# Block sums on GpSimd, stores in other queues, later seeds: an attention and gated-MLP kernel

## The chip, the cores and the metric

One core of a Trainium2 chip runs the whole kernel. The metric is the device time of one execution in microseconds, the median of several runs. The kernel runs five engines beside each other: TensorE (PE, matmuls), VectorE (DVE), ScalarE (ACT), GpSimd (POOL) and SyncE (SP). DMAs are issued by SP, ACT or POOL, each in the order in which they stand on that engine.

## The reference

The output mixes an attention branch s and a gated MLP branch g: `x + s * g`. All data is fp32, 2048 rows by 512 columns.

```python
xn = _layernorm(x, axis=-1)
s = _A_ref(xn, A_wqkv, A_wo)      # 32 heads of 16; each row attends to 8 rows, 2 apart
g = _silu(_B_ref(xn, B_w_in, B_w_sp, B_b_sp, B_w_out))
return x + s * g

# _B_ref
z = _gelu(jnp.einsum("bsd,df->bsf", x, w_in))          # w_in: 512 x 1792
z1 = z[..., :Fh]                                       # Fh = 896
z2 = _layernorm(z[..., Fh:], axis=-1)
g = jnp.einsum("ts,bsf->btf", w_sp, z2) + b_sp[None, :, None]   # w_sp: 2048 x 2048
return jnp.einsum("bsf,fd->bsd", z1 * g, w_out)
```

## The kernel before

**Precision.** Each fp32 operand is split into a high half (ScalarE copies it, L192, tile names end in h) and a low half (VectorE subtracts, L193, names end in l). A product takes three matmuls: high by high, high by low, low by high (L709 to 711, L801, L1036 to 1038).

**Stages of TensorE**, in order: q, k, v (to about 141 us of the span); z1 (first half of w_in, to 226); z2 (second half, the "second projection", to 300); the spatial product of w_sp and z2 (to 582); the projection b by w_out (to 658); the projection s of the attention's output by wo (to 706).

**The spatial product** is done by blocks with seven instead of eight products, each for two column halves of the output (a = 0, 1): m1, m2, m6, m7, m4, m5, m3. `block_product` goes over 8 row blocks of weights, two in a step, and after a step runs what `steps` lists. Weights are rows of w_sp as they are (`plain`, tiles wsp_*) or sums of blocks (`summed`, tiles ws_*) that were stored earlier to sums_d. A product adds onto PSUM banks that ScalarE seeds with a bias or with minus an earlier product (`seed`, L819).

**The block sums** come in eight sets (1, i) of interest here. In the kernel before, GpSimd adds sets 0 to 4 early, in the qkv stage (`pool_sums`, L389, loads and stores through its own queue). VectorE adds sets 5 and 6 in the z2 stage (`raw_sums`, tiles sr_*, their buffers shared with the raw weights, four in all; loads by SP, stores by ACT). GpSimd adds set 7 in m1a (`late_sums`).

**z2 stage.** Per row block j: gelu from PSUM into a tile zt_j (ScalarE, L712), statistics (VectorE, L721), reciprocal deviation (GpSimd, L723 to 726), normalisation (ScalarE, L730), split. `combine` (L743) then takes differences of the tiles zt_i and zt_(i+8) and stores two pieces to t_d, L749 and L750, read back later as operands of m4 to m7. The zt tiles share eight buffers with block sums and others (`t4`): a new tile waits for the last reader of the old one, a store too. In the program as built zt_10 follows zt_0 in one buffer.

**Attention** runs on VectorE through nearly the whole span, 16 units of two steps (products L561 and L605, reductions L568). GpSimd does the first fold of each (L616) and stores the result to o_d (L630). `load_o` brings it back as tiles ol_g_k, four pieces each, split into o_k for the projection s.

**What sets the order.** A framework schedules the program from priorities and its own cost estimates; it fixes the order on each engine before the run. `pin` keeps some instructions in program order. A change in one place can therefore move instructions elsewhere. The gates z1 * g are stored to g_d (`stored_gates`) and read back ahead of the projection b.

Of the kernel before, what the change touches and what calls it, by code (L numbers as in the profile page):

```python
# [57 lines left out]
def kernel(  # L58
# [12 lines left out]
):  # L71
    nc = tc.nc
    pins = [True]
    lows, sums_of = [], []

    def pin(ins):
        return tc.keep_in_program_order(ins) if pins[0] else ins
# [112 lines left out]

    def split(hi, lo, src):
        first_ = pin(nc.scalar.activation(hi, src, AF.Copy))  # L192
        lows.append(pin(nc.vector.tensor_tensor(lo, src, hi.bitcast(F32), op=ALU.subtract)))  # L193
        return first_

# [205 lines left out]
    def raw_sums(a, i):  # L401
        ts = [
            fetch(w_sp[2 * a + c, r + i], CT, f"sr_{a}_{i}_{c}_{r}") for r in (0, HT) for c in range(2)
        ]
        added(ts, nc.vector)
        for n, t in enumerate(ts):
            nc.scalar.dma_start(sums_d[a, n // 2, i, :, n % 2], t)

    def early_tile(name):
        return t2(name).rearrange("p (i t) -> p i t", i=2)  # L410
# [63 lines left out]
    for j in range(11, NT):  # L474
        if j + 2 < NT:
            fetch_cols(j + 2)
        turned = column_tile(j)
        if j == 12:
            for i in range(HT - 3):
                pool_sums(1, i, early_tile, turned, SYNC)  # L480
        low_x(j - 1, cols[j - 1])
        if j % 2:
            pair(0, j - 5)
# [233 lines left out]
    def z2_stats(j, zt):  # L717
        st = const.tile([P, 2, 6], F32, tag="st2", name=f"zst_{j}", bufs=3)
        mv, nm = mvz[:, j], nmz[:, j : j + 1]
        for h in range(2):  # L720
            nc.vector.bn_stats(st[:, h], zt[:, h * FQ : (h + 1) * FQ])  # L721
        nc.vector.bn_aggr(mv, st)
        nc.gpsimd.tensor_tensor(nm, mv[:, 0:1], mone, op=ALU.mult)  # L723
        nc.gpsimd.tensor_scalar(mv[:, 1:2], mv[:, 1:2], EPS, None, op0=ALU.add)
        nc.gpsimd.tensor_tensor(mv[:, 1:2], mv[:, 1:2], nhalf, op=ALU.pow)
        return nc.gpsimd.tensor_tensor(nm, nm, mv[:, 1:2], op=ALU.mult)  # L726

    def z2_normal(j, zt, n):
        zh, zl = z2_at(j)
# [5 lines left out]
    def combine(i, zts):  # L735
        b11, b12, b21, b22 = [z[:, p_] for z in zts for p_ in (first_part, last_part)]
        for out_, p_, q_, op in (
            (b11, b11, b12, ALU.subtract),
            (b12, b12, b22, ALU.subtract),
            (b22, b22, b11, ALU.add),  # L740
            (b21, b21, b22, ALU.subtract),
        ):
            nc.vector.tensor_tensor(out_, p_, q_, op=op)  # L743
        split(*[t[:, ODD + 1 :] for t in z2_at(i)], blocks(b22, ODD))
        v = b11
        src = bass.AP(
            tensor=v.tensor, offset=v.offset, ap=[list(v.ap[0]), [FH - F3, 2], [1, F3]]
        )
        nc.scalar.dma_start(t_d[:2, i].rearrange("a p t -> p a t"), src)  # L749
        nc.scalar.dma_start(t_d[2, i], b21)  # L750

    early_pair = [wts.tile([P, CT], F32R, tag=f"w{n}", name=f"wsp_0_0{n}") for n in "hl"]
    split(*early_pair, fetch(w_sp[0, 0], CT, "wsp_0_0"))
# [6 lines left out]
    raw_z = {}  # L760
    for i in range(HT + 2):
        if i in (1, 3):
            raw_sums(1, HT - 3 + i // 2)
        if i < HT:
            raw_z[i] = [t4(f"zt_{j}").rearrange("p i t -> p (i t)")[:, :FH] for j in (i, HT + i)]
            for h in range(2):
                for j, zt in zip((i, HT + i), raw_z[i]):
                    z2_half(j, h, zt)
                if i == HT - 1 and h == 0:
                    spatial[0, 1] = spatial_block(0, 1)  # L770
        if 0 < i <= HT:
            for j, zt in zip((i - 1, HT + i - 1), raw_z[i - 1]):
                rows_known = z2_stats(j, zt)
        if i > 1:
            for j, zt, n in zip((i - 2, HT + i - 2), raw_z[i - 2], (ODD + 1, FB)):
                z2_normal(j, zt, n)
            combine(i - 2, raw_z[i - 2])

    def load_o(g, k, i=None):
        ot = raws.tile([P, D], F32, tag="raw", name=f"ol_{g}_{k}", bufs=RAW)  # L780
        for q in range(P // Q):
            a, b = divmod(q, CS // Q)
            pin(nc.sync.dma_start(
                ot[q * Q : (q + 1) * Q].rearrange("c (a x) -> c a x", a=P // Q),
                o_d[2 * k + a, g, :, b].rearrange("(a c) x -> c a x", c=Q),
            ))
# [29 lines left out]
        banks[a, f] = mm(f"g_{a}_{f}")  # L816

    def seed(a, f, src, scale=1.0):
        nc.scalar.activation(banks[a, f], src, AF.Copy, scale=scale)  # L819

    def evict(a, f, out_):
        nc.scalar.activation(out_, banks[a, f], AF.Copy)
# [25 lines left out]
    def summed(a, half_, i):  # L848
        return lambda s: prep(sums_d[a, half_, s, :, i], CT, f"ws_{a}{half_}{i}_{s}")
# [26 lines left out]
    def later(fn, *args):  # L876
        return lambda: fn(*args)
# [5 lines left out]
    def stored_gates(a, f0):  # L883
        zl = z1_pair(2 * a, f0, 2)
        n = min(2, ODD - f0)
        xl = t4(f"xl_{a}_{f0}", n)
        nc.sync.dma_start(xl, x_d[a, f0 : f0 + n].rearrange("f p t -> p f t"))
        for f in (f0, f0 + 1):
            times(zl[:, f - f0], banks[a, f], zl[:, f - f0])
            if f < ODD:  # L890
                seed(a, f, xl[:, f - f0], -1.0)
        nc.scalar.dma_start(g_d[a, f0 : f0 + 2].rearrange("f p t -> p f t"), zl)

    def gated(c, f, src, zt):
        times(zt, src, zt)
# [58 lines left out]
        for f in range(ODD + 1):  # L954
            seed(1, f, biases[1][0])

    def late_sums(i):
        return later(pool_sums, 1, i, t4, rows_known, NOSYNC)

    block_product(  # L960
        0, "m1a", at(0, 0), plain(0, 0, 0), odd(0),
        steps=(
            [second_bias, late_sums(HT - 1)], [], [second_seeds], []
        ),
    )
    oo = t4("oo")
# [2 lines left out]
    def kept(a):  # L969
# [14 lines left out]
    )  # L984
    stored_gates(0, 0)
    stored_gates(0, 2)
    block_product(1, "m2b", at(1, 0), plain(1, 0, 1), odd(1))
    stored_gates(1, 0)
    stored_gates(1, 2)
    block_product(  # L990
        0, "m6a", at(0, LAST), summed(0, 0, 0), steps=([T4[0]], [T4[1]], [T4[2]], [T4[3]])
    )
    spill(0)
    block_product(1, "m6b", at(0, LAST), summed(1, 0, 0))
# [147 lines left out]
```

## Time and profile before

| | |
|---|---|
| time, median of 3 runs | 709.67 us (707.76 to 713.64) |
| the profiled execution | 712.41 us, span 710.6 us, mean granted clock 0.992 |
| PE busy | 693.5 us (98%), 3084 matmuls |
| DVE busy | 610.0 us (86%), 878 |
| ACT busy | 284.3 us (40%), 458 |
| POOL busy | 216.7 us (30%), 246 |
| DMA | 182.38 MB, mean 257 GB/s |

Times in rows of the profile are microseconds from the start of the span. A row of the timeline gives start, duration, engine, line, operation and tiles (buffer numbers left out), and in brackets how long the engine stood idle before it and what ended that. A row of waits gives who waited for whom: total, times, longest. L12 is line 12 of the kernel before.

### The profile page before, as it was taken

To read this page: it belongs to the slowest core of one execution; us is meant where nothing else is said; L and a number is where in the kernel's file an instruction comes from. 1 tells how busy PE (TensorE), PEld (TensorE's weight loads), DVE (VectorE), ACT (ScalarE), POOL (GpSimd) and SP (SyncE) were. 2 spreads that over 40 slices of the span, in tenths; PEclk is the share of its full clock that TensorE was granted. 3 is DMA by queue.
4 is the path that set the end of the run, shared out by engine and by line. 5 is a ranking of instruction groups with operands and counts; after the bars stand their busy time and mean duration, and the time that the engine had idled before them with its cause. 6 is when DMAs were issued, how large, how long until landed. Compare 5 with 4: busy or idle time off the path is not lost.

```text
span 710.6 us, 9238 instructions
## 1 busy us (share of the span) xinstructions
PE 693.5 (98%) x3084; PEld 575.9 (81%) x3084; DVE 610.0 (86%) x878; ACT 284.3 (40%) x458; POOL 216.7 (30%) x246
## 2 busy tenths in 40 slices
PE   8999999999999989989999989999999999999996
PEld 7888888888888979967788878888888888888885
DVE  6775387998999999997999999999998999997445
ACT  4343332332433463865444435432343453213421
POOL 3104594522334557536122112142210111320000
PEclk9999999999999999999999999999999999999998
DMA  8759999879999672556798858576659675444896
GB/s 267 257 182 339 337 371 338 249 222 396 310 397 390 233 255 83 180 201 237 264 383 315 312 171 295 194 247 231 217 186 310 189 240 196 151 168 140 281 294 240
DMA packets 106177, 182.38 MB, mean 257 GB/s; under 512 B 9168, under 2 KB 49360, under 8 KB 106128
## 3 DMA queue, kind: packets, MB, share of 16 engines
q1 hardware_dynamic: 56608, 97.42, 40.8%
q0 software_dynamic: 12224, 48.05, 19.4%
q10 hardware_dynamic: 37296, 36.31, 15.0%
q8 instruction: 24, 0.39, 0.2%
q14 instruction: 25, 0.20, 0.1%
HBM read 122.42 MB, written 59.32 MB: 256 GB/s over the span
## 4 chain that ended last, share of the span: by engine, by line
PE 55%; DVE 18%; DMA 14%; issue 7%; ACT 3%; POOL 1%; SPq 1%; ACTq 0%; DVEq 0%
PE g L801 25%; PE qkv L383 5%; PE qkv L381 5%; PE qkv L382 5%; PE b L1038 3%; PE b L1037 3%; PE b L1036 3%; DVE lg L568 3%; DMA sg<-b_d 3%; DVE pr L561 2%; DMA x<-in_x 2%; DMA z_d<-z1t 2%; DVE BIG L193 2%; DVE pv L605 2%; DMA sb<-in_w_sp 1%
## 5 line engine op out<-in xcount | busy, mean ns | idle before, releaser
L616 POOL TENSOR_TENSOR pv<-pv 128x1024 f32<-128x1024 f32 x29 | 69.6, 2399 | 87.9 <-DVE pv L605 87.9
L561 DVE TENSOR_TENSOR pr<-k,q 128x2048 f32<-128x2048 f32 x32 | 74.3, 2322 | 8.9 <-DMA q<-qkv_d 5.3
L605 DVE TENSOR_TENSOR pv<-v,lg 128x2048 f32<-128x2048 f32 x32 | 73.2, 2287 | 1.4 <-DMA v<-qkv_d 0.9
L568 DVE TENSOR_REDUCE lg<-pr 128x128 f32<-128x2048 f32 x32 | 72.9, 2278 | 0.1
L630 POOL DMA_DIRECT2D o_d<-tt x32 | 18.0, 564 | 175.5 <-DVE tt L629 175.3
L429 ACT ACTIVATE stage<-qkv 128x512 f32<-128x512 f32 x36 | 21.4, 596 | 49.5 <-PE qkv L383 44.6
L709 PE MATMUL z<-w_0h,BIG 128*128 128x512 f32 x64 | 25.8, 403 | 2.2 <-ACT zt L712 2.2
L621 DVE TENSOR_TENSOR pv<-pv 128x512 f32<-128x512 f32 x32 | 22.9, 715 | 3.6 <-POOL pv L616 3.5
L710 PE MATMUL z<-w_0l,BIG 128*128 128x512 f32 x64 | 25.7, 401 | 0.0
L730 ACT ACTIVATE zt<-zt,nmz,mvz 128x896 f32<-128x896 f32 x16 | 18.0, 1132 | 19.0 <-POOL nmz L726 18.9
L711 PE MATMUL z<-w_0h,BIG 128*128 128x512 f32 x64 | 25.5, 399 | 0.0
L540 POOL DMA_DIRECT2D k<-qkv_d x13 | 7.3, 560 | 55.6 <-DVE pr L561 55.6
L276 DVE TENSOR_TENSOR xT<-xT,mr 128x512 f32<-128x512 f32 x20 | 13.8, 688 | 11.7 <-DMA mr<-mv_d 6.9
L1047 ACT ACTIVATE bt<-b 128x512 f32<-128x512 f32 x16 | 9.5, 596 | 33.5 <-PE b L1038 33.5
L710 PE MATMUL z<-w_1l,BIG 128*128 128x384 f32 x64 | 21.6, 337 | 0.7 <-DVE w_1l L193 0.7
L192 ACT ACTIVATE BIG<-zl 128x512 fp32r<-128x512 f32 x20 | 12.4, 628 | 24.4 <-DVE zl L871 24.4
L193 DVE TENSOR_TENSOR BIG<-zt,BIG 128x512 fp32r<-128x512 f32 (+2 forms) x24 | 19.8, 826 | 2.4 <-ACT BIG L192 2.4
L711 PE MATMUL z<-w_1h,BIG 128*128 128x384 f32 x64 | 21.5, 336 | 0.0
L709 PE MATMUL z<-w_1h,BIG 128*128 128x384 f32 x64 | 21.5, 335 | 0.0
L389 POOL TENSOR_TENSOR sb<-sa,sb 128x512 f32<-128x512 f32 x12 | 16.8, 1402 | 11.3 <-DMA sb<-in_w_sp 10.9
L801 PE MATMUL g<-ws_1h,BIG 128*128 128x512 f32 x52 | 20.1, 389 | 0.0
L801 PE MATMUL g<-ws_3h,BIG 128*128 128x512 f32 x52 | 20.1, 389 | 0.0
(475 smaller groups left out, 2304.5 us busy)
## 6 DMA issues: line engine op xcount, KB each, us to landing
qkv_d<-stage ACTq DMA_DIRECT2D x24, 512.0 KB
v<-qkv_d POOLq DMA_DIRECT2D x14, 704.0 KB, 4.9
k<-qkv_d POOLq DMA_DIRECT2D x13, 704.0 KB, 5.9
sums_d<-sa POOLq DMA_DIRECT2D x14, 512.0 KB, 6.4
sums_d<-sb POOLq DMA_DIRECT2D x14, 512.0 KB, 7.3
z_d<-z1t ACTq DMA_DIRECT2D x14, 512.0 KB
zl<-z_d SPq DMA_DIRECT2D x12, 512.0 KB
tr<-t_d SPq DMA_DIRECT2D x12, 384.0 KB
```

The source lines that it names most:

```text
L193: lows.append(pin(nc.vector.tensor_tensor(lo, src, hi.bitcast(F32), op=ALU.subtract)))
L381: nc.tensor.matmul(pq, xh[:, k], wh, start=k == 0, stop=False)
L382: nc.tensor.matmul(pq, xh[:, k], wl, start=False, stop=False)
L383: nc.tensor.matmul(pq, xl[:, k], wh, start=False, stop=k == KB - 1)
L561: line(nc.vector.tensor_tensor(pr, taps(ks[u], j0), qb.unsqueeze(1).to_broadcast([P, W, NJ * CS]), op=ALU.mult))
L568: line(nc.vector.tensor_reduce(lgs[u][:, :, j0 * HS : (j0 + NJ) * HS], pr.rearrange("p w (i d) -> p w i d", d=DH), axis=AX.X, op=ALU.add,))
L605: line(nc.vector.tensor_tensor(pv.rearrange("p w (i d) -> p w i d", d=DH), taps(vs[u], j0).rearrange("p w (i d) -> p w i d", d=DH), lgs[u] ...
L616: eng.tensor_tensor(pv[:, 0:4], pv[:, 0:4], pv[:, 4:8], op=ALU.add)
L709: nc.tensor.matmul(pz, xh[:, k], wh, start=k == 0, stop=False)
L710: nc.tensor.matmul(pz, xh[:, k], wl, start=False, stop=False)
L711: nc.tensor.matmul(pz, xl[:, k], wh, start=False, stop=k == KB - 1)
L801: nc.tensor.matmul(pg, z[a], w[b], start=start and i == 0, stop=stop and i == 2, skip_group_check=seeded)
```

## The change

Three things:

1. GpSimd adds six sets early instead of five; VectorE adds sets 6 and 7 in the z2 stage; the late set on GpSimd, and the tiles it took, are gone.
2. Stores move between queues: those of `raw_sums` (8) and of `combine` (16) from ACT's to SP's, those of `stored_gates` (4) from ACT's to GpSimd's. Of the four loads of each ol tile, two move from SP's to GpSimd's queue.
3. The seeds of `stored_gates` are collected and issued in step 2 of the next block product, ordered behind the last high half that was split by then.

```diff
-    lows, sums_of = [], []
+    lows, highs, sums_of = [], [], []
@@ split
         first_ = pin(nc.scalar.activation(hi, src, AF.Copy))
+        highs.append(first_)
@@ raw_sums
-            nc.scalar.dma_start(sums_d[a, n // 2, i, :, n % 2], t)
+            nc.sync.dma_start(sums_d[a, n // 2, i, :, n % 2], t)
@@ the qkv stage
-            for i in range(HT - 3):
+            for i in range(HT - 2):
                 pool_sums(1, i, early_tile, turned, SYNC)
@@ combine
-        nc.scalar.dma_start(t_d[:2, i].rearrange("a p t -> p a t"), src)
-        nc.scalar.dma_start(t_d[2, i], b21)
+        nc.sync.dma_start(t_d[:2, i].rearrange("a p t -> p a t"), src)
+        nc.sync.dma_start(t_d[2, i], b21)
@@ the z2 loop
-            raw_sums(1, HT - 3 + i // 2)
+            raw_sums(1, HT - 2 + i // 2)
@@ load_o
-            pin(nc.sync.dma_start(
+            pin((nc.gpsimd if b else nc.sync).dma_start(
@@ stored_gates
             if f < ODD:
-                seed(a, f, xl[:, f - f0], -1.0)
-        nc.scalar.dma_start(g_d[a, f0 : f0 + 2].rearrange("f p t -> p f t"), zl)
+                awaited.append((a, f, xl[:, f - f0], -1.0))
+        nc.gpsimd.dma_start(g_d[a, f0 : f0 + 2].rearrange("f p t -> p f t"), zl)
+
+    awaited = []
+
+    def seeds():
+        for args in awaited:
+            tc.add_manual_dep(
+                seed(*args).ins, highs[-1].ins.name, NOSYNC, reason="behind the weights"
+            )
+        awaited.clear()
@@ the block products
-            [second_bias, late_sums(HT - 1)], [], [second_seeds], []
+            [second_bias], [], [second_seeds], []
...
-    block_product(1, "m2b", at(1, 0), plain(1, 0, 1), odd(1))
+    block_product(1, "m2b", at(1, 0), plain(1, 0, 1), odd(1), steps=([], [seeds], [], []))
...
-        0, "m6a", at(0, LAST), summed(0, 0, 0), steps=([T4[0]], [T4[1]], [T4[2]], [T4[3]])
+        0, "m6a", at(0, LAST), summed(0, 0, 0),
+        steps=([T4[0]], [T4[1], seeds], [T4[2]], [T4[3]]),
```

In the changed program as built zt_11 follows zt_0 in one buffer, and zt_10 follows sa_0_7, a tile of the block sums (0, i).

How the order moves is shown at three places. In the names, numbers behind the last underscore only count tiles.

The start of m1a, on TensorE (g_0_0 and g_0_1 are its first two column blocks, wsp_0_s its weights, L951, now L961, writes zeros for m1b). Before, the one group ran on to the sixth weight:

```order
L801 MATMUL g_0_0_3224<-wsp_0_4l_3313,BIG_98 128x512
L801 MATMUL g_0_0_3224<-wsp_0_4h_3312,BIG_98 128x512
L951 MATMUL g_1_2_3230<-BIG_98 128x512
L801 MATMUL g_0_0_3224<-wsp_0_5h_3318,BIG_98 128x512
L801 MATMUL g_0_1_3225<-wsp_0_0h_2474,BIG_98 128x512
L801 MATMUL g_0_1_3225<-wsp_0_0l_2475,BIG_98 128x512
```

```order
L802 MATMUL g_0_1_3235<-wsp_0_4h_3312,BIG_98 128x512
L802 MATMUL g_0_0_3234<-wsp_0_4l_3313,BIG_98 128x512
L802 MATMUL g_0_0_3234<-wsp_0_4h_3312,BIG_98 128x512
L802 MATMUL g_0_1_3235<-wsp_0_4l_3313,BIG_98 128x512
L802 MATMUL g_0_1_3235<-wsp_0_4h_3312,BIG_98 128x512
L961 MATMUL g_1_3_3241<-BIG_98 128x512
L802 MATMUL g_0_0_3234<-wsp_0_5h_3318,BIG_98 128x512
L802 MATMUL g_0_1_3235<-wsp_0_5h_3318,BIG_98 128x512
```

Now the second column block takes its first five weights ahead of the first matmul with wsp_0_5h. On ScalarE the seed of g_0_1 and the two gelus of zt_15 have moved ahead of the split of wsp_0_5, and the table load and the exponential of lg_6 behind it. In SP's queue the stores of t_d and of the sums now stand between the loads of these weights.

The end of m2b on VectorE (ws_100_s are m6b's weights, pv_8_0 and lg_9 the attention's). Before:

```order
L599 TENSOR_TENSOR lg_8_1509<-lg_8_1509,sm_8_1575 128x256
L605 TENSOR_TENSOR pv_8_0_1579<-v_4_0_1573,lg_8_1509 128x2048
L568 TENSOR_REDUCE lg_9_1553<-pr_9_4_1566 128x8x16
L583 MEMSET lg_9_1553 1x8
L583 MEMSET lg_9_1553 1x16
L193 TENSOR_TENSOR ws_100_0l_4041<-ws_100_0r_4038,ws_100_0h_4040 128x512
L193 TENSOR_TENSOR ws_100_1l_4047<-ws_100_1r_4044,ws_100_1h_4046 128x512
```

```order
L194 TENSOR_TENSOR ws_100_0l_4041<-ws_100_0r_4038,ws_100_0h_4040 128x512
L194 TENSOR_TENSOR ws_100_1l_4047<-ws_100_1r_4044,ws_100_1h_4046 128x512
L630 STREAM_TRANSPOSE tt_7_4_1580<-pv_7_4_1571 128x256
L598 TENSOR_REDUCE sm_8_1585<-lg_8_1519 128x32
L599 RECIPROCAL sm_8_1585<-sm_8_1585 128x32
L600 TENSOR_TENSOR lg_8_1519<-lg_8_1519,sm_8_1585 128x256
L606 TENSOR_TENSOR pv_8_0_1589<-v_4_0_1583,lg_8_1519 128x2048
L569 TENSOR_REDUCE lg_9_1563<-pr_9_4_1576 128x8x16
```

The low halves of the first two weights now stand ahead of the product and the reduction.

The end, in SP's queue (ol_2_* is the last group of the attention's output, out stores results). Before:

```order
L783 DMA ol_2_2_6092<-o_d_84 32x4x128 x4
L783 DMA ol_2_3_6101<-o_d_84 32x4x128 x3
L1097 DMA out_0<-sg_4_5898 128x1024
L1059 DMA x3_10_6040<-in_x 128x1024
L783 DMA ol_2_3_6101<-o_d_84 32x4x128
L1097 DMA out_0<-sg_6_5933 128x1024
```

```order
L784 DMA ol_2_2_6092<-o_d_84 32x4x128 x2
L784 DMA ol_2_3_6101<-o_d_84 32x4x128 x2
L1105 DMA out_0<-sg_2_5858 128x1024
L1067 DMA x3_8_6005<-in_x 128x1024
L1066 DMA sg_10_6039<-b_d_76 128x1024
L1105 DMA out_0<-sg_4_5898 128x1024
```

SP's two pieces of ol_2_3 now stand ahead of two more stores of results; its other two are in GpSimd's queue, behind the attention's last store.

More of the change, by code (lines that the diff above doesn't have):

```diff
@@ L725, in z2_stats @@
         nc.gpsimd.tensor_tensor(mv[:, 1:2], mv[:, 1:2], nhalf, op=ALU.pow)
-        return nc.gpsimd.tensor_tensor(nm, nm, mv[:, 1:2], op=ALU.mult)
+        nc.gpsimd.tensor_tensor(nm, nm, mv[:, 1:2], op=ALU.mult)
     def z2_normal(j, zt, n):
@@ L772 @@
             for j, zt in zip((i - 1, HT + i - 1), raw_z[i - 1]):
-                rows_known = z2_stats(j, zt)
+                z2_stats(j, zt)
         if i > 1:
@@ L818, in seed @@
     def seed(a, f, src, scale=1.0):
-        nc.scalar.activation(banks[a, f], src, AF.Copy, scale=scale)
+        return nc.scalar.activation(banks[a, f], src, AF.Copy, scale=scale)
     def evict(a, f, out_):
@@ L955, in second_seeds @@
             seed(1, f, biases[1][0])
-    def late_sums(i):
-        return later(pool_sums, 1, i, t4, rows_known, NOSYNC)
     block_product(
```

## The prediction

> **What bounds the kernel now.** I read the page first, then the waits of PE, then the slices in which PE stood still, then the rows around each stall.
>
> ```profile
> PE 693.5 (98%) x3084; PEld 575.9 (81%) x3084; DVE 610.0 (86%) x878; ACT 284.3 (40%) x458; POOL 216.7 (30%) x246
> PE g L801 <- ACT wsp_5h L192: 2.4, 1, 2.4
> ...
> PE g L801 <- DVE ws_0l L193: 2.2, 1, 2.2
> PE g L801 <- ACT wsp_7h L192: 1.0, 1, 1.0
> ```
>
> TensorE is busy 98% of the span and the change takes no matmul away, so only time in which PE waits or runs slowly can be won. Its waits behind the opening are a handful: four of 2.2 to 2.4 us (two more of them stand in the brackets of rows below) and one of 1.0. The slices show that a wait costs more than itself (columns: width, then PE, PEld, DVE, ACT, POOL busy with counts, granted clock, DMA share, GB/s).
>
> ```profile
> 260.00:270.00 10.00, 7.81 (x32) 6.52 (x31) 8.88 (x14) 5.58 (x11) 3.99 (x4) 0.83 0.47 173
> 300.00:310.00 10.00, 7.60 (x28) 5.78 (x28) 10.00 (x13) 9.94 (x17) 3.78 (x4) 0.86 0.53 172
> 350.00:360.00 10.00, 10.00 (x45) 8.29 (x45) 9.97 (x12) 7.57 (x13) 1.50 (x2) 1.00 1.04 349
> 410.00:420.00 10.00, 7.84 (x35) 6.18 (x34) 9.00 (x14) 3.91 (x7) 2.37 (x1) 1.00 0.62 195
> ```
>
> Undisturbed, 45 matmuls of 512 columns start in 10 us, one each 0.222 us. Behind the waits at 260 and 304 us the granted clock falls to 0.83 and 0.86 and matmuls start further apart; behind the one at 411 us it stays 1.00.
>
> ```profile
> 260.12 0.39 PE L711 MATMUL z<-w_0h,BIG 128*128 128x512 f32 x1
> 262.70 0.80 PE L709 MATMUL z<-w_0h,BIG 128*128 128x512 f32 x1 [2.19 <-ACT zt L712]
> ...
> 266.22 0.40 PE L711 MATMUL z<-w_0h,BIG 128*128 128x512 f32 x1
> 304.24 0.39 PE L951 MATMUL g<-BIG 128*128 128x512 f32 x1
> 307.03 0.76 PE L801 MATMUL g<-wsp_5h,BIG 128*128 128x512 f32 x1 [2.40 <-ACT wsp_5h L192]
> ...
> 310.60 0.39 PE L801 MATMUL g<-wsp_2l,BIG 128*128 128x512 f32 x1
> 411.26 0.84 PE L801 MATMUL g<-ws_0h,BIG 128*128 128x512 f32 x3
> 414.26 0.50 PE L801 MATMUL g<-ws_0l,BIG 128*128 128x512 f32 x1 [2.16 <-DVE ws_0l L193]
> 692.97 0.39 PE L1038 MATMUL s<-BIG,o_2l 128*128 128x512 f32 x1
> 695.54 0.50 PE L1036 MATMUL s<-BIG,o_3h 128*128 128x512 f32 x1 [2.18 <-ACT o_3h L192]
> ...
> 699.75 0.40 PE L1037 MATMUL s<-BIG,o_2h 128*128 128x512 f32 x1
> ```
>
> Nine starts from 260.12 to 266.22 should take 9 x 0.222 = 2.0 us and take 6.10: 4.1 lost in the second projection. Nine from 304.24 to 310.60: 4.4 lost in the first block product, m1a. Three from 411.26 to 414.26: 2.3 lost in m6b. Eleven from 692.97 to 699.75: 4.3 lost in the last projection, s. With the 1.0 us for wsp_7h that is 16.1 us, or 2.3% of the kernel. Beyond waits under 1 us, the change cannot bring more than this, whatever else it moves.
>
> **Second projection.** What is late at 262.70 is a gelu, and the gelu waits for its tile:
>
> ```profile
> 256.20 0.55 DVE L743 TENSOR_TENSOR zt<-zt,zt 128x384 f32<-128x384 f32 x1
> 256.78 0.38 ACTq L749 DMA_DIRECT2D t_d<-zt  x1
> 262.05 0.60 ACT L712 ACTIVATE zt<-z 128x512 f32<-128x512 f32 x1 [4.69 <-DMA t_d<-zt]
> 270.00:280.00 10.00, 10.00 (x52) 9.02 (x51) 10.00 (x27) 4.87 (x7) 6.69 (x12) 1.00 0.37 120
> ```
>
> PE's matmul at 262.70 wants the bank that zt_10's gelu at 262.05 empties. zt_10 has zt_0's buffer, so that gelu waits until VectorE has combined zt_0 (done 256.75), the store is issued (256.78) and has landed (5.2 us later). The store left ScalarE's queue 0.03 us after VectorE was done: the queue delayed nothing here, and moving the store alone brings nothing. What brings something is the tile: in the changed program zt_11 takes zt_0's buffer, and zt_10 that of a set of sums stored well before. zt_11's bank is wanted one round of 48 matmuls later; 52 start in 10 us there, so 9.2 us later, at 269.3 if nothing stalls at 260. VectorE now puts zt_0's second difference behind an attention product and a reduction (2.29 and 2.28, rows of m6b below), so the store may land 4.6 later, at 266.6, and the gelu is done at 267.2, still 2.1 early. ScalarE's normalisations stand behind that gelu, though, and the next tiles hang on them: I take -3.1; the ends are 0 (the stall comes back whole a round later) and -4.1.
>
> **First block products.** The high half of the sixth weight is the late one:
>
> ```profile
> 304.75 1.28 ACT L591 ACT_TABLE_LOAD   x1
> 306.36 0.61 ACT L192 ACTIVATE wsp_5h<-wsp_5r 128x512 fp32r<-128x512 f32 x1
> 306.88 0.58 ACT L819 ACTIVATE g<-b_a 128x512 f32<-128x512 f32 x1
> 309.33 0.98 ACT L712 ACTIVATE zt<-z 128x512 f32<-128x512 f32 x2
> 298.07 0.33 SPq L169 DMA_DIRECT2D wsp_5r<-in_w_sp  x1
> SPq L169 <- DMA sums_d<-sr_0r: 46.5, 3, 23.6
> ```
>
> PE wanted it at 304.5 and ScalarE, busy 9.94 of 10 in that slice, made it at 306.36, behind an exponential and its table load (1.6 us from 304.75). In the changed order two things stand otherwise. PE takes 16 more matmuls (the second column block with the weights before) ahead of the first one with wsp_5h: 16 x 0.222 = 3.6 us, so it wants wsp_5h at 308.1. ScalarE has its split ahead of the table load, but the seed of that column block (0.58) and two gelus (0.98) now ahead of it: the same 306.4. So the gap of 2.4 goes, and with it the slow matmuls. Next in line is the seed of the third column block, now behind the table load, the exponential and one more split: 306.4 + 0.6 + 1.7 + 0.6 + 0.6 = 309.9, where PE comes to it six matmuls behind 308.1, at 309.4. Some 0.5 us, with slow matmuls 1.1, come back: -3.3, between 0 and -4.4. That weights and raw sums share four buffers, and SP stood up to 23.6 us behind the landing of sums, I count at nothing: VectorE adds two sets as before, at the same places. The short stalls at 323 to 346 us I leave too, though GpSimd no longer adds there beside VectorE:
>
> ```profile
> 329.58 2.37 DVE L193 TENSOR_TENSOR BIG<-zt,BIG 128x896 fp32r<-128x896 f32 x1
> 331.07 2.03 POOL L389 TENSOR_TENSOR sa<-sa 128x512 f32<-128x512 f32 x1
> ```
>
> This low half, 896 wide, takes 2.37 beside GpSimd's add; by the 0.92 of the 512 wide one in m6b below it would be 1.6, so some 0.8 us of VectorE come back with this one instruction. For PE that lies between 0 and the 1.0 of wsp_7h; I take 0, since the next thing late is not in these rows.
>
> A rule speaks about the clock. The Trainium skill (TensorE: Matmul & The Clock Gate, Part 1) has the clock halved only after about 3.4 us without work, in windows that run free. The trace differs: waits of 2.19 and 2.40 us were enough for slices at 0.83 and 0.86, and one of 2.16 was not. By that rule the two stalls above would be worth their gaps alone, 4.6 us instead of 8.5, and the sum would be some 3 us less.
>
> **m6b.**
>
> ```profile
> 408.84 2.29 DVE L605 TENSOR_TENSOR pv<-v,lg 128x2048 f32<-128x2048 f32 x1
> 411.05 2.28 DVE L568 TENSOR_REDUCE lg<-pr 128x128 f32<-128x2048 f32 x1
> 413.29 0.92 DVE L193 TENSOR_TENSOR ws_0l<-ws_0r,ws_0h 128x512 fp32r<-128x512 f32 x1
> ```
>
> The low half of m6b's first weight stands behind two attention operations of 2.3 us. In the changed order it stands ahead of them, with its neighbour: -2.3, if the load is there; the ends are 0 and -2.3. The seeds behind the next weights cost nothing themselves: eight copies on an engine that is 40% busy. The four stores of gates from GpSimd's queue cost 4 x 0.54 us there (the issue at 651.56 below), between folds.
>
> **Last projection.** The last piece of the fourth o tile is issued late:
>
> ```profile
> 683.84 1.59 SPq L783 DMA_DIRECT2D ol<-o_d  x2
> 688.01 0.80 SPq L783 DMA_DIRECT2D ol<-o_d  x1
> 694.86 0.63 ACT L192 ACTIVATE o_3h<-ol 128x512 fp32r<-128x512 f32 x1 [6.13 <-DMA ol<-o_d]
> 651.56 0.54 POOL L630 DMA_DIRECT2D o_d<-tt  x1 [5.14 <-DVE tt L629]
> ```
>
> At 688.01 the piece stands behind stores of results that wait for ScalarE and VectorE. Now half of these loads go through GpSimd's queue, which has nothing else to do after 651.56, and SP's half stands ahead of those stores: two of the four pieces, issued by 684.6. It took 6.85 from the issue to the split at 694.86 and 0.68 from there to PE's matmul: 692.1, and PE is ready at 693.2. Margin 1.1 us, so I take -3.5. The ends are -4.3 and +2: GpSimd's folds now stand behind o loads that wait for the landing of o_d, and what that shifts of the attention's tail comes into s if it uses up the 32 us between 651.56 and 683.84.
>
> **Opening.** The sixth set on GpSimd is four adds, two loads and two stores in front of the attention's folds.
>
> ```profile
> 125.36 1.76 DVE L621 TENSOR_TENSOR pv<-pv 128x512 f32<-128x512 f32 x1 [3.54 <-POOL pv L616]
> 165.82 1.29 DVE L389 TENSOR_TENSOR sb<-sa,sb 128x512 f32<-128x512 f32 x2 [3.38 <-DMA sb<-in_w_sp]
> ```
>
> By the add of 2.03 above and a DMA issue of 0.54, 4 x 2.0 + 4 x 0.5 = 10 us of GpSimd; VectorE already waited 3.54 for a fold beside the fifth set. It may wait as long again, and 3.38 of its idle time at 165.8 takes that up. I count +1, ends 0 and +3.5.
>
> **Sum.** -3.1 - 3.3 - 2.3 - 3.5 + 1 = -11.2. A reordered VectorE that is 86% busy will be late somewhere else; I set +2 for one short stall of the 1.0 us kind with its slow matmuls or two without. That is -9.2. The profiled execution took 712.41 (span 710.6), 2.7 above the median of 709.67 (707.76 to 713.64); the terms are stalls that I take to be in all of them, so 709.7 - 9.2 = 700.5.
>
> **Rivals.** *A: the front gives nothing.* VectorE is at 10.00 in the slices at 270 and 300, and at 260 it lacks about what PE's stall took from it. If tiles and weights there end in VectorE's work, which is not less, then each stall that goes comes back at the next tile, and m6b's weight, put ahead of the attention, waits for its load. Left are -3.5 and +1: 707.2. Against it: the stalls at 262 and 307 were released by ScalarE, with VectorE's part done.
>
> *B: a queue is worth its issue only.* The store of zt_0 landed when VectorE was done plus 5.2 us, and would through any queue. If o loads too are bound by the transfer, the -3.5 goes; weights then come no earlier, m1a's and m6b's terms fall with them, and -3.1 for the tile and +1 stay: 707.6. For it: the 0.03 us above. Against it: 688.01, where the order in one queue was late, not the transfer. The Trainium skill (DMA: Bandwidth & Descriptors, Issuing engines are not separate DMA queues) states this rule: transfers share the same engines whoever starts them, and another starter saves the time of issue. The trace agrees at 256.78 and not at 688.01.
>
> *C: slower, by SP's queue.* On SP the stores that wait for VectorE now stand between loads of weights: t_d of zt_3, zt_4 and zt_11 ahead of wsp_5, zt_12 ahead of the bias and m1b's weights, zt_5, zt_6, zt_13 and zt_14 further on. Each holds every load behind it until VectorE has combined, and one attention operation in front of that is 2.3 us, as long as the gap that cost 4.4. From three such stalls on it decides: with the front's gain gone, 707.2 + 3 x 4.4 = 720.4 (two give 716.0). For it: SP loaded just in time (298.07 for a split at 306.36). Against it: in the changed order of VectorE the differences of zt_3, zt_4 and zt_11 stand a dozen rows and more ahead of wsp_5's split.
>
> **Chances.** The forecast 0.56, with a range of its own of 694 to 705, A 0.15, B 0.10, C 0.19. Some 1%, or 7.1 us, is about what a measurement of this kernel can tell from no change: below 702.6 faster, above 716.8 slower. Of the forecast 0.51 lies below 702.6 and 0.05 within; A and B are within but for 0.03 faster; C is 0.16 slower and 0.03 within. So 0.54, 0.30 and 0.16. The range from 694 to 715 leaves out most of C and the 0.03 in which every term reaches its end.
>
> **What would show it.** In the profile after: no wait of zt on t_d above 2 us near 262 and slice clocks of 1.00 there; wsp_5h's split ahead of the exponential with no wait of PE for it, 44 or more matmuls in each 10 us slice to 350; ws_0l ahead of the attention's product in m6b; no wait for o_3h. SP rows of t_d in which loads of wsp follow within 1 us speak against C. The prediction is wrong if PE's waits in 260 to 350 sum to as much as before, if waits for wsp weights grow in number, or if DVE's tail delays the start of s beyond its shift.

## The result

The changed kernel takes 706.97 us (median of 20 runs, 701.77 to 710.30), the kernel before 710.9 us beside it (20 runs, 707.76 to 713.66). The ratio is 0.9937, 95% interval 0.9917 to 0.9957: faster by 0.6%, where 1.3% was forecast. Four of the 20 executions took 701.8 to 702.7 us, the others 705.3 to 710.3; the profiled one (707.69) is of the second kind. The profiled execution has a span of 705.9 us, 4.7 less than before. The first view, PE's waits (behind the opening there are no others), shows what became of the five stalls the forecast rested on:

```profile
PE z L710 <- ACT zt L713: 3.7, 1, 3.7
PE z L711 <- DVE w_1l L194: 2.8, 1, 2.8
PE z L710 <- ACT w_1h L192: 1.9, 1, 1.9
```

All five are gone: no wait for a gelu at 262 us, none for wsp_5h or wsp_7h, none for ws_0l, none for o_3h. In their place stand two stalls, at other places, the first of two waits. The slices show where (the first two are of the kernel before, the others of the changed one; width; PE, PEld, DVE, ACT, POOL busy; granted clock, DMA share, GB/s):

```profile
220.00:230.00 10.00, 9.28 (x47) 8.11 (x46) 9.86 (x13) 2.87 (x6) 3.83 (x5) 1.00 1.03 404
280.00:290.00 10.00, 10.00 (x52) 9.02 (x51) 8.22 (x13) 6.40 (x11) 7.13 (x9) 1.00 0.32 116
...
220.00:230.00 10.00, 5.32 (x24) 4.31 (x23) 9.89 (x17) 2.31 (x5) 2.71 (x5) 0.88 1.03 387
260.00:270.00 10.00, 10.00 (x52) 9.03 (x51) 9.57 (x14) 7.22 (x11) 8.09 (x8) 1.00 0.68 238
280.00:290.00 10.00, 6.29 (x24) 5.12 (x23) 8.45 (x15) 5.68 (x10) 5.39 (x5) 0.78 0.52 165
300.00:310.00 10.00, 10.00 (x52) 8.94 (x51) 8.10 (x16) 7.68 (x15) 1.90 (x4) 1.00 0.42 155
410.00:420.00 10.00, 10.00 (x46) 8.29 (x45) 9.90 (x15) 3.77 (x7) 2.97 (x2) 1.00 0.74 267
```

The slices at 260, 300 and 410 us, disturbed before, are full at clock 1.00. Those at 220 and 280 hold 24 matmuls where 47 and 52 stood. Adding up for each trace what PE's starts lose against 0.226 us for 512 columns and 0.173 for 384: before 0.8 at 225 us, 4.1 at 260, 4.3 at 304, 2.3 in three short ones up to 346, 2.4 at 411 and 4.3 at 693, together 18.2; after 6.7 at 224 to 234, 6.7 at 282 to 292 and 0.4 at 328, together 13.8. The difference, 4.4, is nearly the span's 4.7.

Not every stall that is gone has lost its cause. At 262 us the gelu for which PE waited starts 0.38 us earlier than before, and the matmul behind it, at 262.70 before, comes only at 265.85 (ScalarE, PE):

```profile
261.67 0.95 ACT L713 ACTIVATE zt<-z 128x512 f32<-128x512 f32 x2
...
265.85 0.39 PE L710 MATMUL z<-w_0h,BIG 128*128 128x512 f32 x1
```

**The stall at 224 us.** The start of the second projection waits for the halves of its own weights, first ScalarE's, then VectorE's (timeline of PE, ScalarE and VectorE):

```profile
226.00 0.45 PE L710 MATMUL z<-w_1h,BIG 128*128 128x384 f32 x1 [1.85 <-ACT w_1h L192]
229.27 0.69 PE L711 MATMUL z<-w_1l,BIG 128*128 128x384 f32 x1 [2.83 <-DVE w_1l L194]
...
223.76 0.63 ACT L692 ACTIVATE z1t<-z1t 128x512 f32<-128x512 f32 x1 [3.58 <-DVE z1t L690]
225.43 0.52 ACT L192 ACTIVATE w_1h<-w_1r 128x384 fp32r<-128x384 f32 x1
...
228.66 0.55 DVE L194 TENSOR_TENSOR w_1l<-w_1r,w_1h 128x384 fp32r<-128x384 f32 x1
```

Both hang on VectorE: ScalarE stood in order behind a z1t that VectorE made late. VectorE is busy 9.89 of 10 us in that slice; it is late from further back. Its timeline in the opening, beside GpSimd's, shows from where:

```profile
130.74 2.48 POOL L390 TENSOR_TENSOR sa<-sa 128x512 f32<-128x512 f32 x1
135.53 3.34 POOL L390 TENSOR_TENSOR sa<-sa,sb 128x512 f32<-128x512 f32 x1
138.95 1.62 POOL L390 TENSOR_TENSOR sb<-sa,sb 128x512 f32<-128x512 f32 x1
...
127.17 2.08 DVE L623 TENSOR_TENSOR pv<-pv 128x256 f32<-128x256 f32 x1
134.29 3.43 DVE L562 TENSOR_TENSOR pr<-k,q 128x2048 f32<-128x2048 f32 x1
137.65 1.77 DVE L622 TENSOR_TENSOR pv<-pv 128x512 f32<-128x512 f32 x1
139.46 1.40 DVE L623 TENSOR_TENSOR pv<-pv 128x256 f32<-128x256 f32 x1
149.02 2.29 DVE L562 TENSOR_TENSOR pr<-k,q 128x2048 f32<-128x2048 f32 x1 [0.39 <-DMA q<-qkv_d]
167.25 0.69 DVE L390 TENSOR_TENSOR sb<-sa,sb 128x512 f32<-128x512 f32 x1 [2.99 <-DMA sb<-in_w_sp]
```

The same four operations in the trace before:

```profile
127.15 0.42 DVE L622 TENSOR_TENSOR pv<-pv 128x256 f32<-128x256 f32 x1
132.61 2.40 DVE L561 TENSOR_TENSOR pr<-k,q 128x2048 f32<-128x2048 f32 x1
134.93 0.68 DVE L621 TENSOR_TENSOR pv<-pv 128x512 f32<-128x512 f32 x1
135.64 0.43 DVE L622 TENSOR_TENSOR pv<-pv 128x256 f32<-128x256 f32 x1
143.76 2.28 DVE L561 TENSOR_TENSOR pr<-k,q 128x2048 f32<-128x2048 f32 x1
```

Beside the sixth set's adds they take 2.08, 3.43, 1.77 and 1.40 us instead of 0.42, 2.40, 0.68 and 0.43: 4.75 us. The attention's seventh product starts at 149.0 instead of 143.8, and VectorE carries these 5 us on to 224 (the twelfth starts at 219.6 instead of 214.2), where PE first needs something of it at once. The idle time on which the prediction counted does not take the lag up: VectorE still waits 2.99 us at 167 for a load, where it waited 3.38 before.

**The stall at 282 us.** A gelu is late again, but not for a tile (PE, ScalarE, GpSimd, VectorE):

```profile
286.37 0.80 PE L710 MATMUL z<-w_0h,BIG 128*128 128x512 f32 x1 [3.71 <-ACT zt L713]
...
284.29 1.13 ACT L731 ACTIVATE zt<-zt,nmz,mvz 128x896 f32<-128x896 f32 x1 [4.61 <-POOL nmz L727]
285.74 1.82 ACT L713 ACTIVATE zt<-z 128x512 f32<-128x512 f32 x4
...
278.58 5.68 POOL L727 TENSOR_TENSOR nmz<-nmz,mvz 128x1 f32<-128x1 f32 x1
285.50 0.19 POOL L727 TENSOR_TENSOR nmz<-nmz,mvz 128x1 f32<-128x1 f32 x1
...
278.46 0.66 DVE L390 TENSOR_TENSOR sr_0r<-sr_0r,sr_8r 128x512 f32<-128x512 f32 x1
279.39 2.27 DVE L562 TENSOR_TENSOR pr<-k,q 128x2048 f32<-128x2048 f32 x1
283.13 1.07 DVE L194 TENSOR_TENSOR BIG<-zt,BIG 128x896 fp32r<-128x896 f32 x1
284.13 0.19 DVE L723 BATCH_NORM_AGGREGATE mvz<-zst 128x2 f32<-128x12 f32 x1
```

A product of 128x1 takes GpSimd 5.68 us here and 0.19 seven us later. It lasts as long as VectorE runs operations with two tiles as input, seven without a break (three of them shown), and ends 0.13 us after VectorE's first one with a single input begins. A normalisation on ScalarE waits for it, and four gelus stand behind that.

### The profile page after: what moved, and what is told of

It reads as the page before. It is cut to its first block, busy times and chain, and to the rows that moved or that the text cites. A ratio compares the mean times of both kernels' runs of the same rounds, so it can differ in the third digit from the quotient of the medians.

```text
span 705.9 us, 9274 instructions
## 1 busy us (share of the span) xinstructions
PE 691.4 (98%) x3084; PEld 577.3 (82%) x3084; DVE 611.1 (87%) x878; ACT 280.6 (40%) x456; POOL 241.5 (34%) x282
## 4 chain that ended last, share of the span: by engine, by line
PE 76%; DVE 8%; DMA 7%; issue 4%; POOL 2%; ACT 1%; SPq 1%; DVEq 0%; ACTq 0%; POOLq 0%
PE g L802 39%; PE qkv L382 5%; PE qkv L384 5%; PE qkv L383 5%; DMA sb<-in_w_sp 4%; PE b L1044 4%; PE b L1045 4%; PE b L1046 4%; PE s L1046 2%; PE s L1044 2%; PE s L1045 2%; DVE lg L569 2%; PE qkv L305 1%; DVE pr L562 1%; POOL nmz L727 1%
## 5 line engine op out<-in xcount | busy, mean ns | idle before, releaser
L1099 DVE TENSOR_TENSOR sg<-s,sg 128x512 f32<-128x512 f32 (+1 forms) x17 | 11.2, 659 | 16.9 <-PE s L1046 16.9
L784 POOL DMA_DIRECT2D ol<-o_d x32 | 17.8, 556 | 20.7 <-DMA o_d<-tt 8.1
L710 PE MATMUL z<-w_1h,BIG 128*128 128x384 f32 x64 | 22.4, 350 | 1.9 <-ACT w_1h L192 1.9
L277 DVE TENSOR_TENSOR xT<-xT,mr 128x512 f32<-128x512 f32 x20 | 13.8, 688 | 10.9 <-DMA mr<-mv_d 6.5
L712 PE MATMUL z<-w_1h,BIG 128*128 128x384 f32 x64 | 22.5, 351 | 0.0
L802 PE MATMUL g<-ws_5h,BIG 128*128 128x512 f32 x52 | 20.3, 390 | 0.0
```

The source lines that it names most:

```text
L710: nc.tensor.matmul(pz, xh[:, k], wh, start=k == 0, stop=False)
L712: nc.tensor.matmul(pz, xl[:, k], wh, start=False, stop=k == KB - 1)
L802: nc.tensor.matmul(pg, z[a], w[b], start=start and i == 0, stop=stop and i == 2, skip_group_check=seeded)
```

## The experiments

Each row is one kernel against the kernel before on the same chip. "7th" and "12th" are the starts of the attention's seventh and twelfth product on VectorE in its profile; "at 224" is what the 80 matmuls from the 961st on took beyond the 16.3 us that they take undisturbed. (The texts of e1 and e2 call the seventh product the sixth, that of e9 calls the twelfth the thirteenth.)

| kernel | median us | ratio, 95% interval | 7th | 12th | lost at 224 |
|---|---|---|---|---|---|
| before (profile of the prediction) | 710.9 | | 143.8 | 214.2 | 1.0 |
| changed | 706.97 | 0.9937, 0.9917 to 0.9957 | 149.0 | 219.6 | 7.5 |
| e1 five sets, rest changed | 699.3 | 0.9864, 0.9804 to 0.9924 | 143.1 | 213.2 | 0.3 |
| e2 six sets, rest as before | 709.34 | 0.9982, 0.9947 to 1.0017 | 147.0 | 216.9 | 1.9 |
| e3 last scale on VectorE | 707.75 | 0.9961, 0.9932 to 0.9991 | 147.4 | 218.8 | 6.4 |
| e4 o loads on SP | 707.32 | 0.9958, 0.9926 to 0.9991 | 150.8 | 223.4 | 9.7 |
| e6 five sets, stores on ACT | 706.62 | 0.9919, 0.9885 to 0.9953 | 143.8 | 218.3 | 6.8 |
| e7 chain broken | 709.43 | 0.9986, 0.9955 to 1.0017 | 147.8 | 217.9 | 4.4 |
| e8 five sets, chain broken | 708.28 | 0.9946, 0.9912 to 0.9980 | 142.1 | 211.9 | 0.0 |
| e9 sixth set not added | 697.64 | 0.9801, 0.9758 to 0.9844 | 141.8 | 212.3 | 0.0 |
| e10 five sets, o loads on SP | 699.96 | 0.9840, 0.9804 to 0.9876 | 143.3 | 213.6 | 1.1 |
| e11 five sets, early seeds | 697.67 | 0.9814, 0.9775 to 0.9852 | 142.0 | 212.1 | 0.0 |
| e12 five sets, rest changed, again | 699.73 | 0.9827, 0.9789 to 0.9864 | 143.1 | 214.0 | 1.5 |

But for e7 to e9, which change the attention's operations or the adds, these kernels are only two programs up to about 246 us. The kernel before, e1, e5, e6, e10, e11 and e12 have one order of operations on all five engines, the changed kernel, e2, e3 and e4 another. So the table holds repeats of one comparison, five sets against six. With six the seventh product starts at 147.0 to 150.8, and the last three of the stretched operations have the same lengths in all four profiles within 0.02 us; with five it starts at 142.0 to 143.8. The loss at 224 is 1.9 to 9.7 with six and 0.0 to 1.5 with five, but for e6. There VectorE became late in another way: behind an early seventh product it waited 6.21 and 2.11 us for loads (at 169 and 206 us), where the kernel before waited 3.38 and 0.94.

**e1, five sets.** In the changed kernel:

```diff
-            for i in range(HT - 2):
+            for i in range(HT - 3):
                 pool_sums(1, i, early_tile, turned, SYNC)
-            raw_sums(1, HT - 2 + i // 2)
+            raw_sums(1, HT - 3 + i // 2)
-            [second_bias], [], [second_seeds], []
+            [second_bias, late_sums(HT - 1)], [], [second_seeds], []
```

> The changed kernel with its first part undone: five sets early on GpSimd, VectorE adds sets 5 and 6, GpSimd the late set in m1a; the queues and the later seeds stay changed. Theory (the sixth set's adds stretch VectorE's two-input operations around 127 to 140 us, VectorE runs 5 us late from 144 us on, and w_1l at the start of z2 pays for it): the sixth attention product starts near 143.8 us and not 149.0, PE loses at most 1 us near 224 us instead of 6.7; time 700 to 703 if nothing else moves. Rival (the stall at 224 us comes from loads that SP now issues late, or from the DMA engines, busy 1.03 of 1 there): the product is early again, yet PE still loses 4 us or more near 224 us; time near 707. Second rival (VectorE's slack at the start of m1a is what removed the stalls there, and the late set takes it back): the stall near 224 goes but those of 2 us and more at 300 to 350 us are back; 705 to 709.

The seventh product starts at 143.1, PE loses 0.3 us at 224, and the median is 699.3. The theory's numbers for the product and the stall hold, and the time is 0.7 below its range; the rival that blamed SP's loads or the DMA engines falls. The second rival is right about the place, though not about its time: between 291 and 318 us PE loses 4.2 us in two stalls (at 298 and 306), about what it lost there before (4.5); whether the late set makes them no run shows.

**e2, six sets alone.** The edit of e1 the other way round, on the kernel before.

> The kernel before with only the first part: six sets early on GpSimd, VectorE adds sets 6 and 7, no late set; queues and seeds as before. Theory: the sixth product starts 5 us later than before (near 149), PE loses 5 to 7 us near 224 us, the end keeps its stall of 4.3 us for o_3h: 712 to 716. Rival (the stall near 224 needs the changed queues): no loss above 2 us near 224, 706 to 709.

0.9982, no difference that can be told. The seventh product is 3.2 us late, but PE loses only 1.9 us at 224, which is the rival's number, and there is no wait for o_3h, so the time stays below what the theory expected. The rival's reason falls all the same: up to 246 us e2 is the same program as the changed kernel, so the smaller loss differs from its 7.5 as one execution from another, not by the queues. With e1, e12 and the changed kernel this gives the square: the first part alone -0.2%, the rest alone -1.4 to -1.7%, both -0.6%. The two do not add; the sixth set takes back 0.7 to 1.1%.

**e3, last scale on VectorE.**

```diff
-        nc.gpsimd.tensor_tensor(nm, nm, mv[:, 1:2], op=ALU.mult)
+        nc.vector.tensor_tensor(nm, nm, mv[:, 1:2], op=ALU.mult)
```

> The changed kernel with one small operation of z2 moved: the last product of the row statistics (128x1, line 727) on VectorE instead of GpSimd. Theory (it took 5.68 us on GpSimd because VectorE ran two-input operations without a break from 278.5 to 284.1, and the normalisation, the gelu behind it and PE waited for it): no wait of 3.7 us for a gelu near 285 us, PE loses at most 2 us in 280 to 295; 700 to 704, the loss near 224 us as it was. Rival (the gelu is late because its tile or ScalarE's order is late anyway): PE still loses 4 us or more in 275 to 300 us; 706 to 708.

The wait for a gelu stays, 3.8 us, and the rival's time, 707.75, comes out. But the trace shows the wait moved, not another cause: now another small product on GpSimd takes it.

```profile
274.26 5.50 POOL L724 TENSOR_TENSOR nmz<-mvz,mone 128x1 f32<-128x1 f32 x1
...
274.42 0.14 DVE L727 TENSOR_TENSOR nmz<-nmz,mvz 128x1 f32<-128x1 f32 x1
279.17 0.54 DVE L744 TENSOR_TENSOR zt<-zt,zt 128x384 f32<-128x384 f32 x1
280.63 0.16 DVE L727 TENSOR_TENSOR nmz<-nmz,mvz 128x1 f32<-128x1 f32 x1 [0.92 <-POOL mvz L726]
```

Its end, 279.76, is the end of VectorE's run of two-input operations (279.71), behind which VectorE itself then waits. PE loses 5.9 us from 270 to 291, not the 2 of the theory.

**e4, o loads on SP.**

```diff
-            pin((nc.gpsimd if b else nc.sync).dma_start(
+            pin(nc.sync.dma_start(
```

> The changed kernel with all loads of the o tiles back in SP's queue. Theory (half the issues in another queue brought the last group early): the last piece is issued behind stores of results again, and PE loses 3 to 5 us near 690 us for o_3h; 710 to 712. Rival (the order in SP's queue alone, which the other changes moved, brought it): no loss there, 706 to 708.

No wait for o_3h: the rival is right, GpSimd's queue is not what brought the end. In SP's order here all four pieces of the last tile stand ahead of the store of results that one of them stood behind before:

```profile
682.99 2.26 SPq L784 DMA_DIRECT2D ol<-o_d  x4
685.29 0.45 SPq L1067 DMA_DIRECT2D x<-in_x  x1
686.30 0.36 SPq L1105 DMA_DIRECT2D out<-sg  x1
```

**e5, the kernel before once more.**

> The kernel before once more, with a second profile. Theory (the stall for o_3h near 693 us is a chance of one execution, since neither the kernel with six sets alone nor the one with the o loads back on SP shows it): no wait for o_3h above 1 us, the stalls at 260 and 304 us (4 us each) and at 411 us (2.4) are there again. Rival (the order of SP's queue at the end makes it every time): a wait of 2 us for o_3h again.

One execution, 710.9 us. The waits for a gelu (2.3 us), wsp_5h (2.8), ws_0l (1.8) and wsp_7h (1.3) are there again, and so is the one for o_3h (1.6). It was no chance: the rival holds. In e2 SP's order has the four pieces ahead of that store too, as in e4, which is why the wait was missing there: the scheduler moved them though the edit is elsewhere.

**e6, five sets and stores on ScalarE's queue.**

```diff
-            nc.sync.dma_start(sums_d[a, n // 2, i, :, n % 2], t)
+            nc.scalar.dma_start(sums_d[a, n // 2, i, :, n % 2], t)
-        nc.sync.dma_start(t_d[:2, i].rearrange("a p t -> p a t"), src)
-        nc.sync.dma_start(t_d[2, i], b21)
+        nc.scalar.dma_start(t_d[:2, i].rearrange("a p t -> p a t"), src)
+        nc.scalar.dma_start(t_d[2, i], b21)
```

> The kernel with five early sets, and the stores of the raw sums and of t_d back in ScalarE's queue; left of the change are the gate stores and half of the o loads on GpSimd and the later seeds. Theory (the stores in SP's queue are what took the stalls near 262 and 307 us away): PE loses 3 us or more each near 262 and in 300 to 312 us, time 704 to 708. Rival (a queue is worth its issue only): the losses there stay under 2.5 us each as with five sets and SP's queue, 698 to 701.

706.62 (705.83 without the profiled execution), against 699.3 and 699.73 with SP's queue: the stores' queue is worth 0.6 to 0.9%. The profiled execution took 713.77 us, 5 us more than the next, and VectorE is late in it at 218 us, so its losses are no measure. What it shows is the order, which is fixed for all executions: on TensorE, VectorE and ScalarE it is that of the kernel before up to 370 us. In m1a the table load and the exponential again stand ahead of wsp_5h's split, and PE waits 2.8 us for it; in m6b the attention's product and reduction stand ahead of ws_1l, and PE waits 2.0 us. So a queue is worth more than its issues, through the order that the scheduler then builds: that rival falls. Of the stall at 262 the trace says nothing, because PE comes there more than 5 us later; the gelu still waits 3.9 us for its store. The 0.8% by which e6 beats the kernel before are not explained but for the wait for o_3h, which it does not have.

**e7, the chain broken.** Two operations of one input around each product of the attention, on a tile of their own:

```diff
+            line(nc.vector.tensor_scalar(brk, brk, 0.0, None, op0=ALU.add))
             line(nc.vector.tensor_tensor(
                 pr, taps(ks[u], j0), qb.unsqueeze(1).to_broadcast([P, W, NJ * CS]), op=ALU.mult
             ))
+            line(nc.vector.tensor_scalar(brk, brk, 0.0, None, op0=ALU.add))
```

> The changed kernel with two tiny VectorE operations of one input (128x1, adding zero to a tile of its own) around each of the 32 products of the attention. Theory (a small GpSimd operation that reads SBUF waits until VectorE comes to an operation that reads only one tile): no GpSimd operation on nmz or mvz longer than 4.5 us in 240 to 300 us where there was one of 5.7, each ends within 0.3 us behind such a VectorE operation, and PE loses at most 4 us in 275 to 295 instead of 6.7; 702 to 706. Rival (they last because of GpSimd itself): one of 5 us again and the loss of 6 us or more; 706 to 709.

The theory fails as it was put, and the rival's numbers come out (709.43, and PE loses 6.8 us from 270 to 291). GpSimd's product still takes 5.14 us, across the new operation:

```profile
276.40 5.14 POOL L731 TENSOR_TENSOR nmz<-nmz,mvz 128x1 f32<-128x1 f32 x1
...
277.21 0.13 DVE L564 TENSOR_SCALAR brk<-brk 128x1 f32<-128x1 f32 x1
277.28 2.27 DVE L565 TENSOR_TENSOR pr<-k,q 128x2048 f32<-128x2048 f32 x1
281.41 0.19 DVE L727 BATCH_NORM_AGGREGATE mvz<-zst 128x2 f32<-128x12 f32 x1
```

Its end did not come at the tensor_scalar of 0.13 us, but at the aggregate of 0.19 us, which began 0.13 before GpSimd was done. Nor does every aggregate end it. In e1 GpSimd's product runs across one and ends at the next:

```profile
276.44 4.26 POOL L727 TENSOR_TENSOR nmz<-nmz,mvz 128x1 f32<-128x1 f32 x1
...
279.44 0.19 DVE L723 BATCH_NORM_AGGREGATE mvz<-zst 128x2 f32<-128x12 f32 x1
280.58 0.19 DVE L723 BATCH_NORM_AGGREGATE mvz<-zst 128x2 f32<-128x12 f32 x1
```

**e8, five sets with the same operations.**

> Five early sets and the same tiny operations on VectorE. Theory: no stall near 224 us, GpSimd's long operation of 4.3 us near 277 is shorter than 3 us, but PE lost only 0.8 us there, so nothing is won: 698 to 701, the 64 operations cost VectorE about 4 us off the path. Rival (VectorE is the bound beside PE, 64 operations come back as stalls): 702 to 705.

708.28: the rival, and worse than it. No stall at 224 us, GpSimd's long operation takes 3.7 us and not less than 3, and there are waits for ws_1l (3.8 us) and others between 374 and 415. That is some 9 us for 64 operations of 0.13; how much of it is their own time on VectorE and how much the order, which they move too, is not shown.

**e9, the sixth set not added.** It leaves out the four adds of set 5 of (1, i), so one set of sums holds raw blocks; its loads and stores stay.

```diff
-        added([top[:, 0], top[:, 1], low[:, 0], low[:, 1]], eng)
+        if (a, i) != (1, 5):
+            added([top[:, 0], top[:, 1], low[:, 0], low[:, 1]], eng)
```

> The changed kernel, but GpSimd leaves out the four adds of the sixth set; its two loads and two stores stay, so one set of sums holds raw blocks. Theory (the adds, through VectorE's stretched operations, make VectorE late): the seventh attention product starts near 143 to 144 us as with five sets, the thirteenth below 215.5, PE loses at most 1.5 us near 224 us; 699 to 703. Rival (the loads and stores, in GpSimd's queue ahead of the attention's own loads or on the DMA engines, make it late): the seventh near 147 or later and 4 us or more lost near 224; 705 to 708.

697.64, ratio 0.9801, and behind the opening PE does not wait at all (all its waits in the profiled execution, span 691.3):

```profile
PE warm L287 <- POOL ident masks.py:199: 1.3, 1, 1.3
PE xt L225 <- DVE mvx L210: 0.4, 1, 0.4
```

VectorE's operations have their old lengths (its timeline; the last row is the seventh product):

```profile
128.13 2.40 DVE L563 TENSOR_TENSOR pr<-k,q 128x2048 f32<-128x2048 f32 x1
130.46 0.68 DVE L623 TENSOR_TENSOR pv<-pv 128x512 f32<-128x512 f32 x1
131.17 0.42 DVE L624 TENSOR_TENSOR pv<-pv 128x256 f32<-128x256 f32 x1
141.80 2.29 DVE L563 TENSOR_TENSOR pr<-k,q 128x2048 f32<-128x2048 f32 x1
```

So it is the adds that stretch VectorE's operations, not the loads, the stores or GpSimd's queue, and without them the stalls at 224 and 282 are both gone. Behind 147 us e9 is not the changed kernel less four adds, though: the scheduler also built another order, on VectorE from there on and on TensorE from 275 us, in m1a too. That PE waits for nothing shows what the kernel can do without the adds, not that the changed kernel's order would do it.

**e10 and e11, two parts taken back with five sets.** e10 has the edit of e4, e11 this one:

```diff
-                awaited.append((a, f, xl[:, f - f0], -1.0))
+                seed(a, f, xl[:, f - f0], -1.0)
```

> Five early sets, the moved stores and the later seeds, with all o loads on SP. In SP's order the last tile's four pieces stand ahead of the third store of results, unlike in the kernel before. Theory (that order, not GpSimd's queue, takes the stall for o_3h away): no such stall, 698 to 701. Rival (GpSimd's queue is needed): PE loses 2 to 4 us near 685 us, 702 to 704.

> Five early sets, all queues as changed, and the seeds back where they were issued before. Theory (the later seeds are worth little): no new stall over 1 us at the turns from m2a to m2b and m2b to m6a or m6b, 698 to 701. Rival (a seed ahead of the next weights on ScalarE holds their high halves back): a wait for ACT or DVE on ws or wsp weights of 1.5 us or more between 365 and 415 us, 701 to 704.

699.96 and 697.67: both inside what five sets give (e12), no wait for o_3h in e10, and one wait of 1.1 us for ws_2l in e11 (e12 has one of 1.0). Half the o loads on GpSimd and the later seeds are worth nothing that can be told beside the moved stores. The gate stores on GpSimd's queue were not tried alone.

**e12, five sets again.**

> Five early sets with everything else of the change, once more in more rounds, against the kernel before on the same chip. If the first four times hold, 699 to 701 and a ratio of 0.983 to 0.988; if VectorE is late by chance in some executions, as it was with the stores on ScalarE, a part of them lies near 706 and the ratio between 0.987 and 0.992.

0.9827 (0.9789 to 0.9864), six times from 695.75 to 702.67, so e1 holds. Five sets with the stores in SP's queue beat both kernels; e11 (0.9814) and e10 (0.9840) cannot be told from it.

## Why the prediction was wrong

The step that failed is the opening, the price of the sixth set: with six sets the kernel gains 0.6%, with five 1.4 to 1.7%. That five sets take 699.7 us for a forecast of 700.5 is luck, for the sum is another. There m1a gains nothing (3.8 to 5.3 us lost from 291 to 318 in e1 and e10 to e12, 4.5 before), where -3.3 was forecast, and the short stalls from 318 to 350, counted at nothing, go (2.4 to 0.1).

- **Opening: predicted +1, ends 0 and +3.5; measured about 6 us at 224.** It priced the sixth set by how long VectorE would wait for a fold and let 3.38 us of idle time take that up. But most of the cost was not a wait: VectorE's own operations grew by 4.75 us beside the adds, and its idle time was still spent on a load (2.99 us at 167). The prediction had rows that say so: a split of 2.37 us beside GpSimd's add for an estimated 1.6, which it used only for the late set that went away, and in the opening a fold of 1.76 us that takes 0.68 at 134.93. A set is four adds wherever it is added. And the lag does not stay where it arises; the next place where VectorE and PE meet without slack was z2's first weights, outside the stretch that was costed.
- **Second projection: predicted -3.1; at 262 us -4.1, at 282 us +6.7.** The gelu no longer waits for a store, but it starts at 261.67, only 0.38 us earlier than before; PE does not wait for it because the stall at 224 brings PE 5.5 us later. What the other tile is worth by itself is not shown. The next limit was named as ScalarE's normalisations, but priced at 1 us; the row of GpSimd's long product stood in the trace before (4.40 us at 279) and was not looked at. With five sets, and in e9, PE loses at most 0.5 us from 270 to 291, in the five profiles with six sets added 1.9 to 6.8; by which way the sixth set does this is open. That GpSimd waits for VectorE is seen in the traces and not shown by an edit, since e3 moved it and e7 did not break it.
- **m1a: predicted -3.3; -4.3, and most of the 2.3 up to 346 too.** The size is near with six sets, but PE comes to m1a 8.3 us later than before, so how much the order did is not shown. With five sets PE waits 1.2 to 1.6 us for a seed there (e1, e10 to e12); a seed is what the prediction named as next in line and priced at 0.5.
- **m6b: predicted -2.3; -2.4.** Right as to the order. e6 adds a reason that was missing: with the stores in ScalarE's queue the scheduler puts a low half, now the second, behind the attention again.
- **Last projection: predicted -3.5; -4.3.** Right in size, and SP's order is the reason; that half of the loads went through GpSimd did nothing beside it (e4, e10).
- **The allowance of +2** was meant for a VectorE that is late somewhere. It was the right worry at a third of its size.
- **Rivals.** The measured 706.97 lies within 1 us of A's 707.2 and B's 707.6, which is luck too. A said that each stall comes back at the next tile; of five one gelu is late again, for another reason, though both new stalls do end in VectorE's work. B falls with e6. C did not occur: PE waits for no wsp weight. The missing rival was a GpSimd that slows VectorE.

## What to carry to other kernels

Work moved to an idle engine is not free if it slows another engine that the critical one needs: look in the trace for the other engine's durations beside such work, and price the move by how far they stretch, at every place where the work is added. Follow a lag of an engine with little idle time to the next place where the critical engine needs it at once; it is paid there, 80 us later here, and idle time spent waiting for a load need not absorb it. A stall that is gone may only have been outrun: check whether the critical engine comes there later. And when several edits come together, time them apart: here the moved stores gave 0.6 to 0.9%, the later seeds and the split loads nothing that can be told, and the sixth set took 0.7 to 1.1% back.

## What the runs showed of the hardware

In these traces GpSimd and VectorE hold each other up. A product of 128x1 on GpSimd took 0.19 us or, in every profiled execution with six sets added and most with five, 3 to 5.7 us, ending with a run of VectorE's two-input operations (279.76 and 279.71 in e3; 284.26 in the changed kernel, where the first one-input operation began at 284.13), or, in e1, at the second one-input operation and not at the first. The other way round VectorE's operation of 0.42 us took 2.08 beside an add. The Trainium skill (SBUF — State Buffer, Who interferes with whom) has the two engines share a pair of ports that one instruction holds to its end, and says that a VectorE instruction with two SBUF inputs contends with a GpSimd instruction that reads SBUF. The traces agree, and show more: GpSimd's operation went on across several VectorE instructions, over runs of 5 us. The same section of the Trainium skill lists tensor_scalar among the operations that can take both ports; whether the 0.13 us operation of e7 failed for that reason no run here shows.

The granted clock fell in slices with waits of 1.9 and 2.8 us (0.88 at 220 us) and of 3.7 us (0.78 at 280), as it did before for 2.2 and 2.4.
